# A planner that lets one engine at a time at a PSUM bank, a query copy moved to ScalarE, and matmuls without readers in TensorE's first waits

## The chip, the cores and the metric

One Trainium2 chip, one of its cores. The metric is the device time of one execution of the whole kernel in microseconds (us); of several runs the median counts.

## The reference, cut to what matters

The kernel computes three layers one after the other on 1536 tokens of width 512 (2 batches of 768): attention with 8 heads of width 64, where a query sees the first 4 keys and a window of 128 keys up to itself; a dense layer with a leaky maximum; and a layer of 8 experts, where each token with a positive skip score goes to the expert with the highest gate logit.

```python
def _attn_ref(q, k, v, n_sink, window):
    scores = scale * np.matmul(q, k.transpose(0, 1, 3, 2))
    ...
    keep = is_sink | in_window
    scores = np.where(keep, scores, -1000000000.0)
    ...
    a = a / (np.sum(a, axis=-1, keepdims=True) + 1e-09)
    return np.matmul(a, v).astype(np.float32)
def _moe_ref(x, w_in, w_out):
    h = x @ w_in
    g = np.maximum(0.01 * h, h)
    return (g @ w_out).astype(np.float32)
def _moe2_ref(x, w_skip, w_gate, w1, w2):
    ...
        h = np.maximum(xc[mask] @ w1[e], 0.0)
        y[mask] = gate_w[mask, None] * (h @ w2[e])
    out[do_compute] = xc + y
```

## The kernel before

**The work.** The tokens are cut into six groups of 256 (`NG`). For each group the heads are taken in four pairs (`KD`), and each pair in two query tiles of 128 (`item`, line 553). The dense layer runs over 16 chunks of 128 hidden columns for each group (`chunk`, line 832), and the attention of group g+1 is worked in between the chunks of group g. At the end come the experts (`plan_routed`, line 1035). Large products are split in a high and a low fp32r part: ScalarE (ACT) copies the high part out of PSUM, VectorE (DVE) subtracts it from the same PSUM tile and so makes the low part. Groups 0 and 1 (`whole`) use plain fp32 in attention, group 2 is `mixed`, groups 3 to 5 use split keys and queries.

**The planner.** The order in which instructions are issued is not that of the code. Every piece of work is an `Op` with an engine, a cost in ns by a small formula (`c_mm`, `c_act`, `c_dve`, lines 24 to 45), a priority, the tiles it reads and writes, and the operations it depends on. `Plan.run` (line 136) simulates the five engines: at each time each free engine takes the ready operation with the lowest priority number whose tiles fit in the free slots (`fits`, line 149). An operation becomes ready a fixed gap after the one it depends on ended: 195 ns after TensorE (PE), 150 ns after another engine. The start order of this simulation is the order in which the instructions are issued; each engine then works its own queue strictly in that order and waits at each instruction for what it needs. Two operations that only read the same tile have no dependency in the planner.

**PSUM.** There are 8 banks, by tag: 2 each for `acc`, `h` and `T`, 1 each for `S` and `PV` (line 245). Each tile of such a tag is one bank. Waits on the chip are put in by the tile framework from the issue order, not by the planner.

**The start.** `constants` (line 1337) runs first and is not in the plan: GpSimd (POOL) makes the identity `idt` and the tile `ones`; DVE waits for the loaded window limits and then makes the masks `mk` in some 13 instructions (lines 1351 to 1391). In the plan, `prep` (line 433) works one pair of group 0: PE transposes the keys into a `T` bank (line 450), ACT copies them out (454, 456), PE transposes the queries into the other `T` bank (460), and the two heads' queries, partitions 0 to 63 and 64 to 127 of that bank, are copied to `qz`, the first by ACT (468), the second by DVE (465, group 0 alone). Then `item` makes the scores (`score`, line 578), DVE masks them with their minimum (585), ACT takes the exponential (588), ACT or POOL divides by the sum (597, 600), PE transposes (616), ACT copies (620), PE multiplies by the values (655).

**Where two engines read one bank.** The query copies of group 0 (465, 468); the keys of groups 3 to 5, two ACT copies and two DVE subtractions (501, 503; `prep_keys`); the transposed weights of groups 2 to 5 (622, 623); the products with the values of groups 2 to 5 (670, 671). `idle` (line 825) already puts such matmuls without readers on the tile `self.spare` at the end of the dense layer:

```python
many = lambda: ones.rearrange("p (o n) -> p o n", o=1).to_broadcast([128, 4, 128])
for _ in range(n):
    self.p.op("PE", 216, lambda: nc.tensor.matmul(out=x.tile.rearrange("p (o n) -> p o n", o=4), lhsT=ones, rhs=many(), start=True, stop=True), w=[x], pr=self.KF * self.NG, after=[done])
```

Of the kernel before, what the change touches and what calls it, by code (L numbers as in the profile page):

```python
# [49 lines left out]


class Buf:
    __slots__ = ("tag", "shape", "dtype", "tile", "left", "state", "first", "loose")

    def __init__(self, tag, shape, dtype):
        self.tag, self.shape, self.dtype = tag, shape, dtype
        self.tile = None
        self.left, self.first = 0, 1 << 60
        self.state = {}


class Op:
    __slots__ = ("i", "eng", "cost", "fn", "pr", "after", "wait", "ready", "bufs", "lat", "start")


class Plan:
# [9 lines left out]
            return 0.0 if a.eng == "PE" else 125.0  # L76
        return 195.0 if a.eng == "PE" else 150.0

    def __init__(self, slots, any_order=()):
        self.any_order = any_order  # L80
        self.slots = dict(slots)
        self.tags = {}
        self.ops = []
        self.keys = {}
        self.gate = {}
# [11 lines left out]
    def op(self, eng, cost, fn, r=(), w=(), pr=0.0, lat=0.0, hold=(), after=()):  # L97

        o = Op()
        o.i, o.eng, o.cost, o.fn, o.pr, o.lat = len(self.ops), eng, cost, fn, pr, lat  # L100
        o.after, o.ready, o.start = [], 0.0, None
        deps, bufs = dict.fromkeys(after), {}
        for items, write in ((r, False), (w, True)):
            for it in items:
                base, sub = it if isinstance(it, tuple) else (it, None)
                if isinstance(base, Buf):
                    bufs[base] = None
                st = self._state(base)
                for s, (wr, rd) in st.items():
                    if sub is None or s is None or s == sub:  # L110
                        deps.update(dict.fromkeys(wr))
                        if write:
                            deps.update(dict.fromkeys(rd))
        for items, write in ((r, False), (w, True)):
            for it in items:
                base, sub = it if isinstance(it, tuple) else (it, None)
                st = self._state(base)
                if write:
                    if sub is None:
                        st.clear()  # L120
                    st[sub] = ([o], [])
                else:
                    st.setdefault(sub, ([], []))[1].append(o)
        deps.pop(o, None)
        o.wait = len(deps)
        for d in deps:
            d.after.append(o)
        bufs.update(dict.fromkeys(hold))
        o.bufs = list(bufs)
        for b in bufs:  # L130
            b.left += 1
            b.first = min(b.first, o.i)
        self.ops.append(o)
        return o

    def run(self, emit_alloc):
# [7 lines left out]
        def later(t, kind, x):  # L144
            nonlocal seq
            seq += 1
            heapq.heappush(future, (t, seq, kind, x))

        def fits(o):
            need = {}  # L150
            for b in o.bufs:
                if b not in taken:
                    if any(live.get(g, 0) for g in self.gate.get(b.tag, ())):
                        return False
                    n = need[b.tag] = need.get(b.tag, 0) + 1
                    if not b.loose and b not in turn[b.tag][0:n]:
                        return False
            return all(free[t] >= n for t, n in need.items())
# [5 lines left out]
        while future:  # L164
            now = future[0][0]
            while future and future[0][0] <= now:
                _, _, kind, x = heapq.heappop(future)
                if kind == "ready":
                    heapq.heappush(ready.setdefault(x.eng, []), (x.pr, x.i, x))
                elif kind == "done":  # L170
                    for d in x.after:
                        d.ready = max(d.ready, now + self.gap(x, d))
                        d.wait -= 1
                        if d.wait == 0:
                            later(d.ready, "ready", d)
                    for b in x.bufs:
                        b.left -= 1
                        if b.left == 0:
                            later(now + 100.0, "free", b)
                elif kind == "free":  # L180
                    free[x.tag] += 1
                    live[x.tag] -= 1
            for eng in sorted(ready):
                if engines.get(eng, 0.0) > now:
                    continue
                q, skipped, got = ready[eng], [], None
                while q:
                    item = heapq.heappop(q)
                    if fits(item[2]):
                        got = item[2]  # L190
                        break
                    skipped.append(item)
                for item in skipped:
                    heapq.heappush(q, item)
                if got is None:
                    continue
                for b in got.bufs:
                    if b not in taken:
                        taken.add(b)
                        if not b.loose:  # L200
                            turn[b.tag].remove(b)
                        free[b.tag] -= 1
                got.start = now
                order.append(got)
                engines[eng] = end = now + got.cost
                later(end, "idle", None)
                if got.lat:
                    dma_free = max(dma_free, now) + got.lat
                later(dma_free + 2000.0 if got.lat else end, "done", got)
# [16 lines left out]
class Arm:  # L226
# [4 lines left out]
    def __init__(self, tc, io, cst, scr, xg, window_attention):  # L231
# [16 lines left out]
        late = {"wm": 4, "xs": 3, "hs": 1, "gT": 1}  # L248
        self.psum_tags = ("acc", "h", "S", "T", "PV")
        self.base, self.attn, self.late = base, attn, late  # L250
        self.p = Plan({**base, **attn, **late}, ("T", "acc"))
        for t in late:
            self.p.gate[t] = tuple(attn)

# [178 lines left out]
    def prep(self, g, qp, p, whole):  # L433
# [21 lines left out]
        if qp == 0:  # L455
# [1 line left out]
        ks = lambda: self.ks[:, p:p + 1, :].to_broadcast([128, 2, 16])  # L457
        P.op("POOL", c_pool1(32), lambda: nc.gpsimd.tensor_scalar(
            out=snk(), in0=ks(), scalar1=1.0, scalar2=1.0, op0=ALU.mult, op1=ALU.mult), r=[("ks", p)], w=[(kT, "s")], pr=pr)
        P.op("PE", 2 * C_TR, lambda: [nc.tensor.transpose(pq.tile[:, j, :], flat("q", 2 * qp + j), idt) for j in range(2)],  # L460
             r=[part("q", 2 * qp + j) for j in range(2)], w=[pq], pr=pr, hold=[kT])
        for h in range(2):
            rows, key = slice(64 * h, 64 * h + 64), [(self.qz, (p % 2, h))]
            if g == 0 and h:
                P.op("DVE", c_dve(256), lambda rows=rows, h=h: nc.vector.tensor_scalar(
                    out=self.qz.tile[rows, p % 2, h, :], in0=pq.tile[rows].rearrange("p j c -> p (j c)"), scalar1=-0.125, scalar2=None, op0=ALU.mult), r=[pq], w=key, pr=pr)
            else:
# [278 lines left out]
    def plan_dense(self):  # L746
# [10 lines left out]
                self.split(self.xr[g, k], (xT, k), lambda i, k=k, xT=xT: xT.tile[:, i, k, :], 256, self.KF * g - 3, "ACT", "DVE")  # L757


        for _ in ahead(0):  # L760
            pass
        inputs(0)
# [36 lines left out]
        self.spare = self.p.buf("acc", [128, 512])  # L799
        self.idle(2, done)  # L800
        self.first_x(x2 + self.gating(g, acc, [1]))

    def first_rows(self):

# [639 lines left out]
```

## Time and profile before

| what | value |
|---|---|
| median of 3 runs | 550.58 us (549.27 to 551.24) |
| the profiled execution | 549.7 us, its span 548.0 us |
| TensorE busy | 517.1 us, 94% of the span |
| VectorE busy | 411.6 us, 75% |
| ScalarE busy | 344.3 us, 63% |
| GpSimd busy | 164.5 us, 30% |
| chain that ended last | PE 74%, DVE 11%, ACT 7%, issue 3% |

All rows are of the one profiled execution; its span runs from the first to the last instruction and is 1.7 us shorter than that execution's device time. Busy time of PE is modelled (matmuls overlap), so a PE that is busy is not one at its peak. An engine's "idle before" is the time in which its queue stood still ahead of an instruction, and the arrow names what ended that time. PEld is the weight load of TensorE, SPq and ACTq are the DMA issues of SyncE and ScalarE.

### The profile page before, as it was taken

Reading aid. Unit: us, or ns where it says so; the run is one execution under the profiler, and the core shown is the slowest. Engines: PE = TensorE matmul, PEld = TensorE weight load, DVE = VectorE, ACT = ScalarE, POOL = GpSimd, SP = SyncE. Lnnn points to the kernel's source line nnn. Section 1 sums busy time; section 2 is a strip of 40 time slices with the busy share of each in tenths; the row PEclk is TensorE's granted clock in tenths of the full one; section 3 lists DMA queues with packets and bytes.
Section 4 is the critical chain, followed back from the end, with each engine's and each line's share of the span. In section 5 each row is a group of like instructions: output and inputs, shape, how many; then the busy total and the mean of one; then the engine's idle time right before and its main releaser. Section 6 shows DMA issues by size and latency. Waiting matters only on the chain.

```text
span 548.0 us, 10288 instructions
## 1 busy us (share of the span) xinstructions
PE 517.1 (94%) x3341; PEld 452.8 (83%) x3341; DVE 411.6 (75%) x1168; ACT 344.3 (63%) x899; POOL 164.5 (30%) x288
## 2 busy tenths in 40 slices
PE   3889999999998999989999999999999999999994
PEld 2779899888887999878988889999998778888883
DVE  4889999998667677687777776675765587788781
ACT  3998865655576556676566676465656377765760
POOL 4332012230155134332433333211131033455331
PEclk9999999999999999999999999999999999999998
DMA  8998443630110211131112230104565359988750
GB/s 158 298 333 279 156 144 97 198 105 25 64 42 22 69 27 42 41 93 35 45 46 50 49 85 18 26 1 178 169 185 191 116 179 372 315 280 300 245 193 19
DMA packets 83806, 72.44 MB, mean 132 GB/s; under 512 B 56563, under 2 KB 64755, under 8 KB 83744
## 3 DMA queue, kind: packets, MB, share of 16 engines
q1 hardware_dynamic: 81456, 70.54, 42.3%
q0 software_dynamic: 1600, 1.04, 0.6%
q8 instruction: 28, 0.46, 0.3%
q14 instruction: 34, 0.28, 0.2%
q10 hardware_dynamic: 688, 0.13, 0.1%
HBM read 65.40 MB, written 10.51 MB: 139 GB/s over the span
## 4 chain that ended last, share of the span: by engine, by line
PE 74%; DVE 11%; ACT 7%; issue 3%; POOL 2%; DMA 2%; POOLq 0%; SPq 0%; ACTq 0%; DVEq 0%
PE h L845 19%; PE acc L866 15%; PE acc L1103 8%; PE h L1086 4%; PE PV L655 4%; PE T L616 3%; PE S L1086 2%; PE PV L1086 2%; PE S L582 2%; DVE C L671 2%; ACT P L588 2%; PE S L866 2%; PE PV L866 2%; DVE kT L503 1%; PE T L1096 1%
## 5 line engine op out<-in xcount | busy, mean ns | idle before, releaser
L845 PE MATMUL h<-x,w 128*128 128x256 f32 x1128 | 154.7, 286 | 0.3 <-DVE x L708 0.2
L845 PEld LDWEIGHTS h<-x,w 128*128 128x128 f32 x1128 | 144.1, 190 | 4.9 <-DVE w L708 0.6
L866 PE MATMUL acc<-w,gh 128*128 128x512 f32 x308 | 100.2, 406 | 0.0
L588 ACT ACTIVATE P<-P,s 128x272 f32<-128x272 f32 (+1 forms) x96 | 50.1, 523 | 27.6 <-DVE s L585 26.2
L600 POOL TENSOR_SCALAR P<-P,s 128x272 f32<-128x272 f32 (+1 forms) x72 | 36.6, 520 | 90.1 <-DVE s L593 77.4
L866 PE MATMUL acc<-w,gl 128*128 128x512 f32 x156 | 61.3, 393 | 0.0
L856 ACT ACTIVATE t<-h 128x256 f32<-128x256 f32 x94 | 35.6, 379 | 38.2 <-PE h L845 37.8
L866 PEld LDWEIGHTS acc<-w,gh 128*128 128x128 f32 x308 | 53.2, 189 | 7.6
L857 DVE TENSOR_TENSOR h<-h,t 128x256 f32<-128x256 f32 x94 | 40.2, 428 | 21.8 <-ACT t L856 21.2
L708 DVE TENSOR_TENSOR w<-wm,w 128x1024 fp32r<-128x1024 f32 x36 | 49.3, 1376 | 3.8 <-ACT w L701 3.2
L701 ACT ACTIVATE w<-wm 128x1024 fp32r<-128x1024 f32 x44 | 45.1, 1057 | 5.1 <-PE h L845 2.9
L859 DVE TENSOR_TENSOR gl<-h,gh 128x256 fp32r<-128x256 f32 x92 | 38.6, 419 | 10.2 <-ACT gh L858 8.9
L858 ACT ACTIVATE gh<-h 128x256 fp32r<-128x256 f32 x92 | 34.9, 379 | 17.4 <-DVE h L857 16.6
L585 DVE CUSTOM_DVE_ANT_0 P<-S,mk 128x272 f32<-128x272 f32 (+1 forms) x70 | 28.9, 413 | 14.7 <-PE S L582 10.2
L701 ACT ACTIVATE w<-wf 128x512 fp32r<-128x512 f32 x52 | 32.0, 626 | 11.1 <-DVE wf L741 8.8
L866 PEld LDWEIGHTS acc<-w,gl 128*128 128x128 f32 x156 | 29.3, 188 | 6.8 <-DVE gl L859 0.2
L708 POOL TENSOR_TENSOR w<-wm,w 128x1024 fp32r<-128x1024 f32 x8 | 19.7, 2461 | 41.8 <-ACT w L701 21.1
L616 PE MATMUL T<-idt,P 128*128 128x128 f32 x152 | 26.9, 293 | 3.8 <-DVE kT L503 2.9
L672 POOL TENSOR_TENSOR xr<-C 128x128 f32<-128x128 f32 x32 | 15.6, 488 | 47.2 <-DVE C L671 46.8
L708 DVE TENSOR_TENSOR w<-wf,w 128x512 fp32r<-128x512 f32 x42 | 28.8, 693 | 0.7 <-ACT w L701 0.7
L616 PEld LDWEIGHTS T<-idt,P 128*128 128x128 f32 x152 | 22.3, 205 | 8.5 <-issue 4.2
L622 ACT ACTIVATE AT<-T 128x256 fp32r<-128x256 f32 x60 | 20.1, 382 | 12.1 <-PE T L616 11.3
(274 smaller groups left out, 1105.9 us busy)
## 6 DMA issues: line engine op xcount, KB each, us to landing
wm<-in_moe_w_dram SPq DMA_DIRECT2D x44, 512.0 KB, 3.8
w<-in_moe_w_in_dram SPq DMA_DIRECT2D x14, 512.0 KB, 7.4
w<-in_moe_w_out_dram SPq DMA_DIRECT2D x14, 512.0 KB, 6.5
wf<-in_moe_w_dram SPq DMA_DIRECT2D x20, 256.0 KB, 4.4
vs<-in_moe_w_dram SPq DMA_DIRECT2D x10, 512.0 KB, 5.7
rq<-in_q_dram SPq DMA_DIRECT2D x56, 64.0 KB, 5.8
out_dram<-x SPq DMA_DIRECT2D x12, 256.0 KB, 2.5
rk<-in_k_dram SPq DMA_DIRECT2D x24, 96.0 KB, 2.2
```

Source lines behind the costliest of these rows:

```text
L588: P.op("ACT", 280 + 0.83 * ncol, lambda h=h: nc.scalar.activation(out=A.tile[:, 0:ncol, h], in_=A.tile[:, 0:ncol, h], func=AF.Exp, scale=- ...
L600: P.op("POOL", 245 + 0.83 * ncol, lambda h=h: nc.gpsimd.tensor_scalar(out=A.tile[:, 0:ncol, h], in0=A.tile[:, 0:ncol, h], scalar1=sm.tile[ ...
L616: nc.tensor.transpose(tt.tile[:, 2 * j + h, :], A.tile[:, o:o + 128, h], c["idt"])
L701: nc.scalar.activation(out=at(0), in_=view(src.tile), func=AF.Copy)
L708: P.op(lo, {"DVE": c_dve(n), "POOL": c_pool2(n)}[lo], lambda: eng[lo].tensor_tensor(out=at(1), in0=view(src.tile), in1=at(0).bitcast(F32), ...
L845: nc.tensor.matmul(out=h.tile, lhsT=wi.tile[:, a, 128 * k:128 * k + 128], rhs=xT.tile[:, b, k, :], start=k == 0 and n == 0, stop=k == self ...
L856: P.op("ACT", c_act(256, True), lambda: nc.scalar.activation(out=t.tile, in_=h.tile, func=AF.Copy, scale=0.01), r=[h], w=[t], pr=fast)
L857: P.op("DVE", c_dve(256), lambda: nc.vector.tensor_tensor(out=h.tile, in0=h.tile, in1=t.tile, op=ALU.max), r=[t], w=[h], pr=fast)
L859: P.op("DVE", c_dve(256), lambda: nc.vector.tensor_tensor(out=gl.tile, in0=h.tile, in1=gh.tile.bitcast(F32), op=ALU.subtract), r=[h, gh], ...
L866: nc.tensor.matmul(out=acc[i].tile, lhsT=a.tile[:, q], rhs=wo.tile[:, b, :], start=first and n == 0, stop=last and n == 2)
L1086: nc.tensor.matmul(out=hp[a].tile, lhsT=xt.tile[:, i, k, :], rhs=w1[k][j].tile[:, 512 * a:512 * a + 512], start=k == 0 and n == 0, stop=k ...
L1103: nc.tensor.matmul(out=yp.tile, lhsT=gt.tile[:, a, 2 * n + j, :], rhs=w2[n][b].tile[:, 512 * j:512 * j + 512], start=n == 0 and j == 0 and ...
```

## The change

Three edits. (1) The planner notes for each tile of a PSUM tag which engine last took it and until when (end plus 195 ns for PE, plus 150 ns for others); an operation of another engine on that tile does not fit before then. Operations that merely reserve a tile (`held`) don't count. (2) For the first pair of group 0 both heads' queries are copied by ACT; for pairs 1 to 3 the second head stays with DVE. (3) A function `warm` puts matmuls of `ones` with itself (bf16, 512 columns) on an `acc` tile that nothing reads: 7 at the head of TensorE's queue, 5 after the first pair's query transposes. The plan counts each at 10 ns.

```diff
 class Plan:
-    def __init__(self, slots, any_order=()):
-        self.any_order = any_order
+    def __init__(self, slots, any_order=(), banks=()):
+        self.any_order, self.banks = any_order, banks
...
+        o.held = set(hold) - set(bufs)
         bufs.update(dict.fromkeys(hold))
...
         def fits(o):
+            if any(b.tag in self.banks and b.by != o.eng and b.until > now and b not in o.held for b in o.bufs):
+                return False
             need = {}
...
                 later(end, "idle", None)
+                for b in got.bufs:
+                    if b.tag in self.banks and b not in got.held:
+                        b.by, b.until = eng, end + (195.0 if eng == "PE" else 150.0)
+                        later(b.until, "idle", None)
...
-        self.p = Plan({**base, **attn, **late}, ("T", "acc"))
+        self.p = Plan({**base, **attn, **late}, ("T", "acc"), self.psum_tags)
...
-        P.op("PE", 2 * C_TR, lambda: [nc.tensor.transpose(pq.tile[:, j, :], flat("q", 2 * qp + j), idt) for j in range(2)],
-             r=[part("q", 2 * qp + j) for j in range(2)], w=[pq], pr=pr, hold=[kT])
+        turned = P.op("PE", 2 * C_TR, lambda: [nc.tensor.transpose(pq.tile[:, j, :], flat("q", 2 * qp + j), idt) for j in range(2)],
+                      r=[part("q", 2 * qp + j) for j in range(2)], w=[pq], pr=pr, hold=[kT])
+        if g == 0 and p == 0:
+            self.warm(5, pr, [turned])
         for h in range(2):
             rows, key = slice(64 * h, 64 * h + 64), [(self.qz, (p % 2, h))]
-            if g == 0 and h:
+            if g == 0 and p and h:
                 P.op("DVE", c_dve(256), lambda rows=rows, h=h: nc.vector.tensor_scalar(
...
+        if self.fast:
+            self.spare = self.p.buf("acc", [128, 512])
+            self.warm(7, -100)

         for _ in ahead(0):
             pass
...
+    def warm(self, n, pr, after=()):
+        nc, ones, x = self.nc, self.c["ones"], self.spare
+        many = ones.rearrange("p (o n) -> p o n", o=1).to_broadcast([128, 4, 128])
+        self.p.op("PE", 10 * n, lambda: [nc.tensor.matmul(out=x.tile.rearrange("p (o n) -> p o n", o=4), lhsT=ones, rhs=many, start=True, stop=True) for _ in range(n)],
+                  w=[x], pr=pr, after=after)
```

## Rows read from the trace of the kernel before

**Rows 1.** Busy time by stage: stretch, length, each engine, PEclk, DMA share, GB/s.
```profile
8.30:20.00 11.70, 9.47 (x51) 7.60 (x52) 6.38 (x32) 8.71 (x33) 2.66 (x9) 1.00 1.08 277
20.00:56.00 36.00, 32.64 (x222) 28.10 (x222) 34.23 (x105) 32.31 (x99) 9.91 (x18) 1.00 1.00 294
56.00:166.00 110.00, 108.78 (x718) 97.25 (x717) 96.25 (x276) 69.63 (x196) 24.67 (x47) 1.00 0.33 101
166.00:380.00 214.00, 206.31 (x1442) 186.41 (x1441) 151.91 (x528) 133.10 (x409) 69.77 (x159) 1.00 0.18 46
```

**Rows 2.** The chain that ended last, its first 13 us: start, us, what.
```profile
0.91 4.07 DMA lim<-in_window_dram
...
8.02 0.30 DVE mk L1391
...
8.35 0.44 DVE w L465
```

**Rows 3.** The timeline of the start: start, us, instruction, idle before it.
```profile
2.24 0.19 POOL L1368 MEMSET ones<- 128x128 bf16 x1
...
5.72 0.99 PE L450 MATMUL T<-idt,w 128*128 128x128 f32 x2 [5.72 <-DMA w<-in_k_dram]
...
6.51 0.63 PE L460 MATMUL T<-idt,w 128*128 128x128 f32 x2
...
7.03 0.18 ACT L456 ACTIVATE ks<-T 128x16 f32<-128x16 f32 x1
...
8.81 0.38 ACT L468 ACTIVATE w<-T 64x256 f32<-64x256 f32 x1 [1.60 <-DVE w L465]
...
9.33 0.77 PE L578 MATMUL S<-kT,w 128*128 128x128 f32 x2 [2.19 <-ACT w L468]
...
10.14 0.29 DVE L585 CUSTOM_DVE_ANT_0 P<-S,mk 128x128 f32<-128x128 f32 x1 [1.36 <-PE S L578]
...
12.13 0.68 PE L450 MATMUL T<-idt,w 128*128 128x128 f32 x4
...
17.89 0.41 DVE L737 TENSOR_SCALAR wf<-w 128x512 int32<-128x512 int32 x1
```

**Rows 4.** Score matmuls to 12.6 us and from 15.5, line 830's (ns min/median/max).
```profile
L578 PE MATMUL S<-kT,w x4: 422/606/661, 9.3 to 11.7; 128*128 128x128 f32 x2, 128*128 128x272 f32 x2
...
L578 PE MATMUL h<-kT,w x6: 275/275/395, 15.7 to 17.8; 128*128 128x128 f32 x4, 128*128 128x272 f32 x2
...
L830 PE MATMUL acc<-ones x7: 376/389/393, 432.8 to 438.4; 128*128 128x512 bf16 x7
...
432.84 0.60 PE L830 MATMUL acc<-ones 128*128 128x512 bf16 x2
```

**Rows 5.** DMA before pair 1's transposes, columns as in rows 1, and the landing of weights.
```profile
10.00:10.50 0.50, 0.50 (x4) 0.50 (x4) 0.30 (x2) 0.03 (x1) 0.00 (x0) 1.00 1.31 208
...
11.00:11.50 0.50, 0.50 (x2) 0.38 (x2) 0.03 (x1) 0.40 (x2) 0.00 (x0) 1.00 0.43 87
...
10.44 0.58 SPq L720 DMA_DIRECT2D w<-in_moe_w_in_dram  x1
...
DMA to landing us min/median/max: 4.7/5.2/5.6
```

**Rows 6.** The timeline where ACT and DVE read one bank in a late group.
```profile
237.32 0.97 ACT L501 ACTIVATE kT<-T 64x384 fp32r<-64x384 f32 x2
238.33 1.12 DVE L503 TENSOR_TENSOR kT<-T,kT 64x384 fp32r<-64x384 f32 x2 [0.18 <-ACT kT L501]
```

**Rows 7.** The waits of PE from 166 to 380 us: us in total, times, longest.
```profile
PE T L616 <- DVE kT L503: 2.9, 7, 0.6
PE T L943 <- DVE wl L933: 1.3, 1, 1.3
PE T L638 <- DVE qT L684: 1.3, 4, 0.6
PE T L494 <- issue: 1.2, 1, 1.2
```

More of the change, by code (lines that the diff above doesn't have):

```diff
@@ L52 @@
 class Buf:
-    __slots__ = ("tag", "shape", "dtype", "tile", "left", "state", "first", "loose")
+    __slots__ = ("tag", "shape", "dtype", "tile", "left", "state", "first", "loose", "by", "until")
     def __init__(self, tag, shape, dtype):
@@ L58, in __init__ @@
         self.left, self.first = 0, 1 << 60
+        self.by, self.until = None, 0.0
         self.state = {}
 class Op:
-    __slots__ = ("i", "eng", "cost", "fn", "pr", "after", "wait", "ready", "bufs", "lat", "start")
+    __slots__ = ("i", "eng", "cost", "fn", "pr", "after", "wait", "ready", "bufs", "lat", "start", "held")
 class Plan:
```

## The prediction

> **What bounds the kernel now.** I read the busy time by stage first. From 56 to 166 us PE is busy for 108.78 of 110 us, from 166 to 380 us for 206.31 of 214 [rows 1]: there the end is set by TensorE's work and by its pauses, 7.7 us of them in the second stretch. Before that it is different. From 8.3 to 20 us no engine is full (PE 9.47 of 11.70, DVE 6.38, ACT 8.71), and from 20 to 56 us DVE (34.23 of 36) and ACT (32.31) are fuller than PE (32.64) [rows 1]. So the first 20 us are a chain of waits and not a full engine; what follows is work that moves as a whole if that chain gets shorter.
>
> Next the chain that ended last, in its first microseconds. It runs from the load of the limits through DVE's masks, which end at 8.02 + 0.30 = 8.32, to DVE's copy of the second head's queries (line 465) [rows 2]; ACT's copy of the first head's (line 468) comes right behind it, at 8.81 [rows 3]. These two copies write different parts of `qz` and only read one bank, yet ACT stood still for 1.60 us until DVE's was done, and the first scores began at 9.33 after PE had waited 2.19 us [rows 3]. So the program serializes readers of a bank, in the order of issue; DVE's copy came first in that order although DVE was busy with masks the planner doesn't know.
>
> The same in the late groups: ACT copies both heads' keys in 0.97 us from 237.32, and DVE's two subtractions, 1.12 us, start at 238.33, after the second ACT copy and not after the first [rows 6]. The planner believes that DVE can start after the first. For TensorE that ends in waits: of those from 166 to 380 us, 2.9 us in 7 places are for these subtractions, to get a free `T` bank, and 1.3 us in 4 for DVE's low part of the queries [rows 7].
>
> **The change part by part.** Sum against the profiled execution, 549.7 us (span 548.0); the median shown, 550.58, lies 0.88 above it.
>
> *The query copy of the first pair.* DVE loses 0.44 us [rows 2], which it did on the path; ACT gains a second copy of 0.38 [rows 3]. The transposes of the queries end at 6.51 + 0.63 = 7.14 and ACT is free at 7.03 + 0.18 = 7.21 [rows 3], so the copies run to about 7.6 and 8.0 instead of 9.2. Head 0's score needs only the first. Behind it nothing on ACT is hurt: its next work, the exponential, waits for DVE anyway.
>
> *The products without readers.* The seven can start when `ones` is made, 2.24 + 0.19 = 2.43 [rows 3], and read no load. Two products back to back take 0.60 us and one 0.389 [rows 4], so each adds 0.21 us at the fast rate. The first score matmuls took 422 ns (128 columns) and 661 (272), from 15.7 us on 275 and 395 [rows 4]: 239 against 120 ns for 144 more columns, twice. The granted clock reads 1.00 in all stretches [rows 1], that is the higher level of 1.2 and 2.4 GHz; the durations say that the first ones ran at the lower. At the slow rate a product adds 0.42 us and seven end at about 5.6. The keys' transposes can't start before 5.72, when the load lands [rows 3], so these seven cost nothing. The five lie between 7.14 and the score: at the fast rate to 8.2, inside the wait of 2.19 us that PE has there now; at the slow rate to 9.24, and the cover is gone. I take the fast rate, as seven products without a gap precede the transposes, where PE before had stood still for 5.72 us. DMA, SP and POOL issue nothing more; the `acc` bank that the products hold is wanted only by line 616, after the exponentials.
>
> *What the start gives.* Score at 8.2, its two matmuls 0.38 us, so DVE's line 585 at about 8.6 instead of 10.14: 1.5 us. The second tile's four matmuls of 272 columns run at the fast rate and save another 4 x 0.23 = 0.9 (272 columns at 120 ns for 144), so 2.4 us at the last score. Pair 1's transposes stand at 12.13 [rows 3]; the load rate falls from 208 GB/s at 10.0 to 87 at 11.0 [rows 5], so their data are in by about 10.5: at most 1.6 us earlier. The first weights are issued at 10.44 and land 5.2 us later [rows 5], 15.6, while DVE's decoding starts at 17.89 [rows 3]: room for 2.2. I take -1.6 us; the ends are -2.4 and 0, the latter if the products cover nothing and the later stages swallow the rest.
>
> Here the Trainium skill can be weighed. The page "PSUM — Partial Sum Buffer", section "PSUM bank collisions raise a hardware error", says that two engines may be in one bank at once when they touch different quadrants of 32 partitions; the two query copies do (0 to 63, 64 to 127). By it the 1.60 us would be no wait of the bank and the start would gain the clock's 0.9 alone, a sum of 548.2; the row shows the wait in this program, so the row decides.
>
> *The planner's exclusion.* It changes no instruction, only the order. A dependency already had the same gaps (195, 150), so only places with two concurrent readers move: 12 pairs of key copies, the four places listed in the kernel's description. Worked for the keys: the planner costs ACT's copy 52 + 0.83 x 384 = 371 ns and DVE's 465. Before, its bank was done at 371 + 150 + 2 x 465 = 1.45 us; now at 2 x 371 + 150 + 930 = 1.82. On the chip it takes 238.33 + 1.12 - 237.32 = 2.13 [rows 6]. The plan was 0.68 short and is now 0.31 short, so somewhat over half of the waits behind it should go: 1.5 of the 2.9 us [rows 7]. The wait for `T` shown as "issue" (1.2) and that for the queries (1.3) may go too, but their causes are other engines' lateness; I count nothing. The floor of this term is -4: 2.9 and half of the other two. Upward nothing excludes a loss, since every later choice of the planner can fall differently: I bound it by half the pauses of the stage with these places, 7.7 / 2 = +3.8.
>
> Sum: 549.7 - 1.6 - 1.5 = 546.6; plus 0.88, a median of 547.5 us.
>
> **The rivals.** A measurement of this kernel tells 0.3% from no change: below 548.9 is faster, above 552.2 slower.
>
> *Only the start counts.* The plan's new order gives back as much as it saves, as every operation behind the first moved one is chosen anew: 550.58 - 1.6 = 549.0. For it: waits other than those for the keys remain, such as 1.3 us for the gating's low part [rows 7].
>
> *The clock comes late.* If PE still runs slowly after the transposes, the five products end at 9.24 and the score starts at 9.3 as now. Only the 0.9 of the second tile is left; with half of the plan's term, 0.75, that is 548.9, without it 549.7. For it: the matmuls from 5.72 to 7.14 before were followed by slow ones [rows 3, 4]. Against it: the products fill the 3 us ahead of that.
>
> The page "TensorE: Matmul & The Clock Gate", Part 1, calls the half rate the default that sustained activity releases, at a point that varies from run to run; that speaks for this case, and the doubled durations agree.
>
> *The start is swallowed.* From 20 to 56 us DVE and ACT are at 95 and 90% [rows 1]; a shorter start could be met there by weights or slots that come no earlier, and the plan's term is nothing: 550.2.
>
> *Slower.* The exclusion holds a `T` bank 0.37 us longer in the plan, and with two such banks the planner puts the transposes of keys and of attention weights later; the attention of the next group then ends after the last chunk of the present one, and the first product of the group (line 845) waits for its input. It decides from 1.1 us per boundary on, in each of groups 3, 4 and 5: at 1.3, as the one gating wait [rows 7], 550.58 - 1.6 + 3.9 = 552.9.
>
> **How the numbers follow.** Forecast 0.52 (its own range 544.5 to 548.9); only the start 0.13, on the border, so half faster; late clock 0.08 and swallowed 0.12, no change; slower 0.15. Faster 0.52 + 0.06 = 0.58, same 0.27, slower 0.15. The range goes down to 550.58 - 2.4 - 4 = 544.2, say 544, and up to 551.5, past the neutral cases; what it leaves out is most of the slower case and a tail below.
>
> **What would show it.** Line 468 without a wait for DVE and done near 8.0; the first line 585 between 8.4 and 8.8; score matmuls of 275 and 395 ns from the first on; pair 1's transposes near 10.5; from 166 to 380 us fewer than 7.7 us of pauses and the wait of line 616 for 503 halved. The forecast is wrong if the start is 1.6 us earlier at 20 us but not at 56, if the first score stays near 9.3, or if PE's pauses after 166 us grow.

## The result, and the profile after

The changed kernel took 543.95 us (median of 4 runs, 541.82 to 544.02) against 550.65 us: the ratio is 0.9869, 95% interval [0.9845, 0.9893], 6.7 us less by the medians and 7.2 by the ratio. Forecast were 547.5 us and a range from 544.0 on: the direction was right, the gain more than twice the forecast one, and the result lies just below the range. The profiled execution took 543.89 us, its span is 542.2 (before 549.7 and 548.0).

Line numbers are higher now: by 8 to 10 up to line 750 (450 is 458, 460 is 468, 465 is 475, 468 is 478, 503 is 513, 578 is 588, 585 is 595, 616 is 626), and by 20 in the dense layer (845 is 865, 859 is 879).

First the busy time by stage of the changed kernel, columns as in [rows 1]; the number in brackets is that of the engine's instructions in the stretch:

```profile
8.30:20.00 11.70, 8.94 (x56) 7.04 (x55) 8.47 (x41) 11.00 (x41) 3.96 (x12) 0.97 1.05 274
20.00:56.00 36.00, 33.64 (x220) 29.05 (x219) 32.72 (x97) 30.83 (x92) 9.37 (x16) 0.96 1.04 310
56.00:166.00 110.00, 108.87 (x729) 98.25 (x727) 96.99 (x281) 69.42 (x197) 27.64 (x50) 1.00 0.32 96
166.00:380.00 214.00, 208.19 (x1465) 189.14 (x1465) 155.50 (x530) 134.41 (x412) 68.83 (x156) 1.00 0.20 52
```

From 166 to 380 us PE's pauses are 214 - 208.19 = 5.8 us instead of 7.7 [rows 1]. More telling is the count: PE worked 1465 matmuls there instead of 1442, and 729 instead of 718 from 56 to 166. It got through 34 more in the same time, while its busy time grew by only 1.9 and 0.1 us.

The start, as the timeline of the changed kernel shows it (start, us, instruction, idle before it):

```profile
2.49 3.17 PE L820 MATMUL acc<-ones 128*128 128x512 bf16 x7 [2.49 <-POOL ones L1388]
5.64 0.36 PE L458 MATMUL T<-idt,w 128*128 128x128 f32 x1
6.42 0.38 PE L468 MATMUL T<-idt,w 128*128 128x128 f32 x2
6.64 1.24 PE L820 MATMUL acc<-ones 128*128 128x512 bf16 x5
6.97 0.77 ACT L478 ACTIVATE w<-T 64x256 f32<-64x256 f32 x2
7.72 0.38 PE L588 MATMUL S<-kT,w 128*128 128x128 f32 x2
7.95 0.30 DVE L1411 TENSOR_SCALAR mk<-mk 128x272 f32<-128x272 f32 x1
8.17 0.28 DVE L595 CUSTOM_DVE_ANT_0 P<-S,mk 128x128 f32<-128x128 f32 x1
9.10 0.60 PE L458 MATMUL T<-idt,w 128*128 128x128 f32 x4
```

ACT copies both heads' queries without a wait; PE begins the first scores at 7.72 instead of 9.33, DVE's line 595 at 8.17 instead of 10.14, pair 1's transposes at 9.10 instead of 12.13 [rows 3]. Line 595 now follows directly on DVE's last mask (L1411). The score matmuls run at the higher rate from the first on; durations (ns min/median/max) of the S bank's first four, where [rows 4] had 422/606/661:

```profile
L588 PE MATMUL S<-kT,w x4: 273/334/393, 7.7 to 8.9; 128*128 128x128 f32 x2, 128*128 128x272 f32 x2
```

The clock's own entries in the traces agree with these durations. The first of them is the rise to the higher level, at 12.3 us in the kernel before and at 5.8 us in the changed one. (A table of stretches prints 1.00 ahead of the first entry too, so it can't show the slow start.)

PE's waits from 166 to 380 us (us in total, times, longest), against [rows 7]:

```profile
PE T L626 <- DVE kT L513: 1.9, 4, 0.8
PE h L865 <- DVE gl L879: 1.3, 2, 1.1
...
PE T L648 <- DVE qT L694: 0.5, 1, 0.5
```

The wait for the keys' subtractions fell from 2.9 us in 7 places to 1.9 in 4, those for the queries' low part at line 648 from 1.3 to 0.5 (with 0.6 at line 592 in addition), and the one marked "issue" is gone. A wait of the dense layer's product (L865) is new: it writes an `h` bank, and waits until DVE has read that bank for the low part of an earlier chunk (L879).

### The profile page after: what moved, and what is told of

It is laid out like the page before. It is cut to its first block, busy times and chain, and to the rows that moved or that the text cites. A ratio compares the mean times of both kernels' runs of the same rounds, so it can differ in the third digit from the quotient of the medians.

```text
span 542.2 us, 10303 instructions
## 1 busy us (share of the span) xinstructions
PE 517.6 (95%) x3353; PEld 453.3 (84%) x3353; DVE 413.3 (76%) x1167; ACT 343.6 (63%) x900; POOL 167.4 (31%) x288
## 3 DMA queue, kind: packets, MB, share of 16 engines
q0 software_dynamic: 1600, 1.04, 0.6%
## 5 line engine op out<-in xcount | busy, mean ns | idle before, releaser
L865 PE MATMUL h<-x,w 128*128 128x256 f32 x1128 | 155.6, 286 | 2.0 <-DVE gl L879 2.0
L865 PEld LDWEIGHTS h<-x,w 128*128 128x128 f32 x1128 | 144.2, 190 | 7.1 <-DVE gl L879 3.2
L610 POOL TENSOR_SCALAR P<-P,s 128x272 f32<-128x272 f32 (+1 forms) x72 | 39.5, 561 | 93.0 <-DVE s L603 75.8
L718 DVE TENSOR_TENSOR w<-wm,w 128x1024 fp32r<-128x1024 f32 x36 | 49.4, 1383 | 2.0 <-ACT w L711 1.7
L879 DVE TENSOR_TENSOR gl<-h,gh 128x256 fp32r<-128x256 f32 x92 | 38.5, 418 | 6.4 <-ACT gh L878 4.8
L718 DVE TENSOR_TENSOR w<-wf,w 128x512 fp32r<-128x512 f32 x42 | 29.2, 702 | 0.7 <-ACT w L711 0.7
L1030 POOL DMA_INDIRECT scr<-x,sm x12 | 13.2, 1098 | 50.6 <-ACT wl L969 16.0
L718 POOL TENSOR_TENSOR w<-wm,w 128x1024 fp32r<-128x1024 f32 x8 | 19.9, 2482 | 28.0 <-ACT w L711 22.0
L626 PE MATMUL T<-idt,P 128*128 128x128 f32 x152 | 25.8, 289 | 1.9 <-DVE kT L513 1.9
```

The lines of the kernel that those rows point to most:

```text
L610: P.op("POOL", 245 + 0.83 * ncol, lambda h=h: nc.gpsimd.tensor_scalar(out=A.tile[:, 0:ncol, h], in0=A.tile[:, 0:ncol, h], scalar1=sm.tile[ ...
L626: nc.tensor.transpose(tt.tile[:, 2 * j + h, :], A.tile[:, o:o + 128, h], c["idt"])
L718: P.op(lo, {"DVE": c_dve(n), "POOL": c_pool2(n)}[lo], lambda: eng[lo].tensor_tensor(out=at(1), in0=view(src.tile), in1=at(0).bitcast(F32), ...
L865: nc.tensor.matmul(out=h.tile, lhsT=wi.tile[:, a, 128 * k:128 * k + 128], rhs=xT.tile[:, b, k, :], start=k == 0 and n == 0, stop=k == self ...
L879: P.op("DVE", c_dve(256), lambda: nc.vector.tensor_tensor(out=gl.tile, in0=h.tile, in1=gh.tile.bitcast(F32), op=ALU.subtract), r=[h, gh], ...
```

## The experiments

Times are medians. The kernel before took between 549.89 and 551.03 us from session to session, so kernels are compared by their ratio to the before of their own session; a difference of 0.1% is 0.55 us.

### The two halves of the change

*Exclusion alone*: products and the query copy taken back.

```diff
-        if g == 0 and p == 0:
-            self.warm(5, pr, [turned])
...
-            if g == 0 and p and h:
+            if g == 0 and h:
...
-            self.spare = self.p.buf("acc", [128, 512])
-            self.warm(7, -100)
```

> The exclusion alone: the query copies of the first pair as before (ACT and DVE), no products without readers. Theory A (the planner's exclusion carries most, the start about 1.9 us of the 6.7): 545.5 to 547.5 us, so 3 to 5 below before, with the first score still at 9.3 and fewer pauses of PE between 166 and 380 us. Rival B (the start and the clock carry most, through everything behind them): 549 to 551.

Measured: 545.43 us, 0.992 [0.9899, 0.9941]. The start is as before: the copies still stand one behind the other, as the timeline of this run shows.

```profile
8.74 0.38 ACT L476 ACTIVATE w<-T 64x256 f32<-64x256 f32 x1 [1.61 <-DVE w L473]
8.86 0.76 PE L586 MATMUL h<-kT,w 128*128 128x128 f32 x2 [1.80 <-DVE w L473]
```

*Start alone*: the exclusion taken back; TensorE's matmuls, other than the products, then run in the order of before.

```diff
-        self.p = Plan({**base, **attn, **late}, ("T", "acc"), self.psum_tags)
+        self.p = Plan({**base, **attn, **late}, ("T", "acc"))
```

> The other two edits without the exclusion. Theory A: 548 to 549.5 us, 1.2 to 2.5 below before. Rival B: 543.5 to 545.5, nearly all of the gain.

Measured: 547.30 us, 0.9948 [0.993, 0.9966]. So the start is worth 0.52%, 2.9 us, and the exclusion 0.80%, 4.4 us; together 7.3, where the whole change gave 7.2 by its ratio. Within the intervals the two halves add up, and the larger one is that which the forecast had at 1.5.

*No products*: the exclusion and the copy, without the twelve products.

```diff
-        if g == 0 and p == 0:
-            self.warm(5, pr, [turned])
...
-            self.spare = self.p.buf("acc", [128, 512])
-            self.warm(7, -100)
```

> The changed kernel without the products that nobody reads (exclusion and both query copies on ACT). Theory A with the clock as the larger part of the start: 545 to 546, 1 to 2 above the changed kernel, the 272-column scores of the first pair at about 660 ns. If the products are worth nothing because the clock falls again at 19.4 us: 543.5 to 544.5. If they are most of the gain: over 547.

Measured: 544.67 us, 0.9896 [0.9879, 0.9914]: 0.15 to 0.27% above the whole change (0.9869, and 0.9881 when it was run again), and 0.24% below the exclusion alone. That lies between the ranges that were expected. By the middle values the products bring about 1 us and the copy about 1.3, but the intervals overlap, so only their sum is settled (the start alone, 2.9).

What the products do to the clock is settled by the traces. Without them its first entry, the rise, stands at 12.3 us (before), 13.3 (exclusion alone) and 17.1 us (no products); in all 17 profiled runs with them it stands between 5.5 and 7.8 us. Where it comes late the five products run slowly themselves and hold the scores up. In the run with ACT's price and the exclusion (below) the rise is at 7.8 us, and the timeline reads:

```profile
6.93 1.68 PE L820 MATMUL acc<-ones 128*128 128x512 bf16 x5
8.45 0.38 PE L588 MATMUL S<-kT,w 128*128 128x128 f32 x2
```

The scores start there 0.7 us later than in the profiled run of the change (7.72), and 0.8 later than in that without products (7.67), whose scores then ran at the lower rate.

### Where the exclusion's time comes from

From 56 to 380 us, one row of the busy time by stage for the kernel before:

```profile
56.00:380.00 324.00, 315.08 (x2158) 283.66 (x2157) 248.16 (x803) 202.74 (x604) 94.44 (x205) 1.00 0.23 65
```

for the start alone:

```profile
56.00:380.00 324.00, 314.93 (x2158) 283.64 (x2158) 247.68 (x801) 202.41 (x601) 94.84 (x205) 1.00 0.24 65
```

and for the whole change:

```profile
56.00:380.00 324.00, 317.07 (x2193) 287.39 (x2192) 252.49 (x810) 203.83 (x609) 96.47 (x205) 1.00 0.24 67
```

An earlier start leaves the pace as it was: 2158 matmuls in these 324 us. With the exclusion there are 35 more. PE's busy time grew by only 2.0 us, but that of its weight loads (the second number, PEld) by 3.7. The groups of instructions say which matmuls came in addition; before:

```profile
L845 PE MATMUL h<-x,w 128*128 128x256 f32 x913 | 125.1, 286 | 0.3 <-DVE x L708 0.2
...
L616 PE MATMUL T<-idt,P 128*128 128x128 f32 x136 | 24.2, 293 | 3.8 <-DVE kT L503 2.9 <-POOL P L600 0.6
```

and after:

```profile
L865 PE MATMUL h<-x,w 128*128 128x256 f32 x936 | 128.9, 286 | 2.0 <-DVE gl L879 2.0
...
L626 PE MATMUL T<-idt,P 128*128 128x128 f32 x136 | 23.2, 289 | 1.9 <-DVE kT L513 1.9
```

The attention's work is the same (136 transposes of weights in both), the dense layer is 23 products further. And the trap of the page can be read here: these products are listed at 286 ns each, but 936 of them at 286 would be 268 us, and the group's busy time is 128.9. A matmul's modelled time overlaps with that of the next, so a wait that is shorter than the overlap would leave no idle time in the table of waits.

How far the dense layer has come shows the gain in time. Durations (ns min/median/max) and the starts of the first and the last product of line 845 in an `h` bank, for the kernel before and for the exclusion alone:

```profile
L845 PE MATMUL h<-x,w x1128: 274/283/485, 25.1 to 423.2; 128*128 128x256 f32 x188
L862 PE MATMUL h<-x,w x1128: 274/283/482, 21.9 to 418.7; 128*128 128x256 f32 x188
```

The last one starts 4.5 us earlier, which is the whole gain; what follows it takes 124.8 and 124.9 us.

The page "Perfetto Trace Analysis" of the Trainium skill, section "Identifying the Most-Contended Engine", says that TensorE's matmul busy share is no good measure, since pipelined matmuls distort it, and advises the rate of the work done and the busy share of its weight loads instead. The traces agree: +2.0 us by the one, +3.7 by the other, 4.4 us measured.

### Rule or luck: five more pairs

One order that is better by 4 us could be luck, since the planner chooses everything behind its first moved operation anew. So its prices were nudged by amounts that mean nothing, each with and without the exclusion (the start edits in all):

```diff
-                            later(now + 100.0, "free", b)
+                            later(now + 130.0, "free", b)
```

> The start edits without the exclusion, and a planner nudged elsewhere: a slot counts as free 130 ns after its last use instead of 100. The nudge moves some 350 lines of TensorE's order and has no meaning of its own. Theory A (the exclusion makes the plan truer, whatever the order around it): 546 to 548.5 us, as the start alone had 547.3. Rival L (the changed kernel's order was a lucky draw and any reshuffle moves the time by some us either way): anything from 543 to 551.

> The changed kernel with the same nudge. Theory A: 3 to 5 us below its partner without the exclusion, so 542 to 545. Rival L: the difference to the partner is anywhere between -4 and +4; under 1.5 would speak for L.

```diff
 def c_dve(n):
-    return 66 + 1.04 * n
+    return 70 + 1.04 * n
```

> The start edits without the exclusion, another nudge: the planner's cost of a VectorE pass is 4 ns higher (70 instead of 66 plus 1.04 per element). Theory A: 546 to 548.5. Rival L: 543 to 551.

> The changed kernel with that second nudge. Theory A: 3 to 5 us below its partner, 542 to 545. Rival L: a difference under 1.5 in this pair or the other, or pairs of opposite sign.

```diff
-C_TR = 114.0
+C_TR = 118.0
```

> A neutral nudge (the planner's price of a transpose 118 ns instead of 114) with the start edits and without the exclusion. Theory A (the exclusion itself saves 3 to 5 us, whatever the order): 546.5 to 550, and 3 to 5 us above its partner with the exclusion. Rival L (the size is the luck of one order): the four orders so far without the exclusion went from 545.4 to 549.9 and those with it from 542.6 to 544.4, so L expects the partners of this pair and of the next to differ by under 2 us, or with the other sign, in at least one of them.

> The same nudge with the exclusion. Theory A: 542.5 to 545, 3 to 5 us below the partner. Rival L: within 2 us of the partner, or above it.

```diff
-    return (52 if psum else 93) + 0.83 * n
+    return (56 if psum else 97) + 0.83 * n
```

> Another neutral nudge (ScalarE's fixed cost 4 ns higher in the planner), without the exclusion. Theory A: 546.5 to 550. Rival L: anywhere from 543 to 550.

> The ScalarE nudge with the exclusion. Theory A: 542.5 to 545, 3 to 5 us below the partner. Rival L: within 2 us of the partner, or above it.

Measured, with PE's matmuls and the weight loads' busy us of 56 to 380 us from the busy time by stage (the last pair is the kernel before and the exclusion alone, times of their session):

| nudge | without: us, ratio | matmuls, loads | with: us, ratio | matmuls, loads | gain |
|---|---|---|---|---|---|
| none | 547.30, 0.9948 | 2158, 283.64 | 543.95, 0.9869 | 2193, 287.39 | 0.79% |
| slot delay | 549.92, 0.9997 | 2150, 282.45 | 544.42, 0.9918 | 2179, 285.64 | 0.79% |
| DVE's price | 545.44, 0.9908 | 2178, 285.30 | 542.63, 0.9872 | 2194, 287.84 | 0.36% |
| transpose's price | 548.36, 0.9953 | 2159, 282.60 | 543.89, 0.9891 | 2185, 287.39 | 0.62% |
| ACT's price | 550.84, 0.9996 | 2158, 283.05 | 545.74, 0.9892 | 2193, 287.37 | 1.04% |
| none, old start | 549.89, 1 | 2158, 283.66 | 545.43, 0.992 | 2193, 287.88 | 0.80% |

All six pairs gain, on average 0.73% or 4.0 us. (In the third the intervals, [0.9888, 0.9928] and [0.9833, 0.9911], overlap.) Rival L's signs, partners within 2 us of each other or a pair of the other sign, show in none. But theory A's figures were too narrow: 549.92, 545.44, 550.84 and 545.74 us lie outside their ranges, and the four nudged pairs differ by 2.8 to 5.5 us. Without the exclusion the orders lie from 545.4 to 550.8 us, with it from 542.6 to 545.7. So the gain is a property of the rule; how much of it one order shows is luck of some 2 us either way. The clock doesn't bring it: the mean granted clock of the timed runs was 0.993 to 0.996 in the kernels with the exclusion and 0.995 to 0.997 in those without. That the gain comes from a plan nearer to the program's waits, and not from something else that holding an engine back does, is argued and not shown.

In the profiled runs of all six pairs the last product of line 845 (865) starts earlier with the exclusion, by 2.3 to 4.9 us. What follows it differs by under 1 us within a pair, except under the slot delay (126.5 us without, where the clock stood at half for 3.4 us from 436.5 us on, and 124.7 with). Two orders without the exclusion took as long as the kernel before (0.9997 and 0.9996). Under ACT's price the start's gain still stands at that product (421.0 us, before 423.2) and is lost behind it, with and without the exclusion alike (127.2 us for the rest, before 124.8).

The pair under the slot delay also shows how little the table of waits tells. PE's wait for the keys' subtractions from 166 to 380 us, without and with the exclusion:

```profile
PE T L626 <- DVE kT L513: 1.4, 3, 0.6
PE T L626 <- DVE kT L513: 3.6, 6, 1.3
```

It grew, PE's busy time from 56 to 380 us went from 315.15 to 314.93 us, and yet 29 more matmuls got through and the kernel was 0.79% faster.

### Which banks

The forecast worked the exclusion for the keys alone, which lie in the T banks. So the rule was given the T tag alone, or the others alone:

```diff
-        self.p = Plan({**base, **attn, **late}, ("T", "acc"), self.psum_tags)
+        self.p = Plan({**base, **attn, **late}, ("T", "acc"), ("T",))
```

> The changed kernel, with the planner's exclusion for the T banks alone (keys, queries and transposed attention weights). If the waits for a T bank are what the exclusion saves: 543 to 545 us, as the changed kernel. If the products with the values (PV, one bank) carry it: 546.5 to 548, as the start edits alone.

```diff
+        self.p = Plan({**base, **attn, **late}, ("T", "acc"), ("PV", "S", "h", "acc"))
```

> The complement: the exclusion for PV, S, h and acc and not for T. If T carries it: 546 to 549. If PV does: 543 to 545. Both low would say that either is enough, or that the order decides more than the place.

and both again under the nudge of DVE's price:

> The exclusion at the T banks alone, under the nudge of DVE's price, whose form without any exclusion took 545.44 us and whose form with all of it 542.63. If T alone carries the gain: 542 to 543.5. If T alone brings nothing (as the run without a nudge said, 550.12): 545 to 550. If the two parts only work together: about 545.4.

> The exclusion at the banks other than T (PV, S, h, acc) under the same nudge. If these carry the gain: 542 to 543.5. If they bring nothing (as the run without a nudge said, 547.0 against 547.3): 545 to 547.

| exclusion at | no nudge | DVE's price |
|---|---|---|
| no bank | 0.9948, 2158 matmuls | 0.9908, 2178 |
| T | 1.0001 [0.9985, 1.0017], 2152 | 0.9985 [0.9966, 1.0003], 2143 |
| the others | 0.9942 [0.9921, 0.9963], 2173 | 0.991 [0.9887, 0.9933], 2172 |
| all | 0.9869, 2193 | 0.9872, 2194 |

The others alone bring nothing, T alone costs 0.53 and 0.77% (2.9 and 4.2 us), and both together gain. The parts don't add up, and T alone came out above every range expected of it, in both runs. The count of matmuls is a guide and no measure: the others alone got 15 more through than the start alone, and their last product of line 865 starts 2.2 us earlier (418.4 against 420.6 us), but what follows takes 1.7 us longer (126.4 against 124.7). With T alone the wait that the forecast priced does shrink, from 2.9 us and, under DVE's price, from 2.2, as PE's waits from 166 to 380 us show in the first of these runs

```profile
PE T L626 <- DVE kT L513: 1.9, 5, 0.6
```

and in the second:

```profile
PE T L626 <- DVE kT L513: 1.2, 3, 0.5
```

Yet both kernels are slower. The timeline of the first shows a place where it goes:

```profile
241.49 0.77 ACT L680 ACTIVATE C<-PV 64x256 f32<-64x256 f32 x2
...
242.28 0.38 ACT L693 ACTIVATE qT<-T 128x256 fp32r<-128x256 f32 x1
...
242.70 0.86 DVE L681 TENSOR_TENSOR C<-PV,C 64x256 f32<-64x256 f32 x2 [0.90 <-ACT qT L693]
243.59 0.42 DVE L694 SCALAR_TENSOR_TENSOR qT<-T,qT 128x256 fp32r<-128x256 f32 x1
...
244.16 0.63 PE L949 MATMUL T<-idt,x 128*128 128x128 f32 x4 [2.13 <-DVE qT L694]
```

DVE's additions for the values (L681) stood still for 0.90 us. They read the PV bank that ACT copies from (the old 670 and 671, a place that T alone doesn't cover). But these copies (L680) ended at 242.26, and the row names as the end of the wait ACT's copy of the queries (L693), which ended at 242.66; why the additions waited for that stays open. The queries' low part (L694) stood behind them in DVE's queue with a T bank in its hands, and PE waited 2.13 us for that bank. The whole change has the same wait of DVE, but PE had products of the dense layer to work on meanwhile:

```profile
239.43 0.88 PE L865 MATMUL h<-x,w 128*128 128x256 f32 x6
...
239.65 0.86 DVE L681 TENSOR_TENSOR C<-PV,C 64x256 f32<-64x256 f32 x2 [0.80 <-ACT qT L693]
```

With T alone, PE's clock fell to half behind that wait, as the busy time by stage shows (the third number from the end):

```profile
241.40:244.20 2.80, 0.67 (x9) 0.52 (x10) 1.60 (x5) 1.21 (x4) 2.27 (x6) 1.00 0.42 94
244.20:245.80 1.60, 0.95 (x7) 0.73 (x8) 0.61 (x3) 1.08 (x3) 1.07 (x3) 1.00 0.02 4
245.80:249.20 3.40, 3.40 (x18) 3.32 (x19) 2.34 (x8) 1.78 (x6) 0.38 (x3) 0.50 0.25 58
```

3.40 us at half the rate is 1.7 us of work lost; with the wait of 2.13 this place alone could account for the 2.9 us by which this kernel is behind the start alone. All its timed runs show the clock: its mean was 0.989 and, under DVE's price, 0.990, where the kernels without any exclusion had 0.996 and 0.997. The difference is 0.0065 in both before rounding, by estimate 0.0065 x 547 = 3.6 us of clock, about as much as the two losses. So T alone may lose by falls of the clock for the most part or wholly; what it would cost without them isn't shown. That the parts need one another because DVE has one queue for all banks fits the place, but isn't shown.

### Is a truer plan always a faster one?

The traces show ACT's and DVE's instructions longer than the planner's prices, and the gaps between engines shorter: a copy and a subtraction of [rows 6] took 485 and 560 ns where the plan has 371 and 465, and DVE began 40 ns behind ACT where it has 150. If the gain came from truth alone, correcting both should add to it:

```diff
+        if a.eng in ("ACT", "DVE"):
+            return 25.0 if a.eng == b.eng else 50.0
...
+        cost += 100.0 if eng in ("ACT", "DVE") and not lat else 0.0
...
-                        b.by, b.until = eng, end + (195.0 if eng == "PE" else 150.0)
+                        b.by, b.until = eng, end + (195.0 if eng == "PE" else 50.0)
```

> The changed kernel with one more truth in the plan: ACT's and DVE's operations cost 100 ns more and the gap behind them is 100 ns shorter, as the trace's durations have it (a 128x384 copy from PSUM takes 483 ns and the plan says 371, while the next engine starts some 45 ns after its end and the plan says 150). Theory A (a truer plan is a faster one): below the changed kernel, 540.5 to 543. Rival L (only the order's luck): 541 to 548 with no preference.

Measured: 575.57 us, 1.0473 [1.0446, 1.0501], outside both ranges. The idea falls in this form. From 166 to 380 us PE got through far less, with waits longer than any that the change has, at a mean clock of 0.95, which by itself is some 10 us of work (0.05 x 214); the row of the stretch, and the two longest waits from 20 to 380 us:

```profile
166.00:380.00 214.00, 195.40 (x1333) 173.51 (x1332) 148.91 (x546) 130.85 (x410) 76.44 (x172) 0.95 0.18 45
```

```profile
PE T L629 <- DVE sAT L655: 3.9, 2, 2.1
PE T L694 <- issue: 3.8, 1, 3.8
```

The kernel's priorities were set with the old prices; why these prices make it so much slower stays open.

### The clock's fall at 19 us

In the profiled run of the change PE waited 1.41 us for POOL, and the granted clock fell behind it:

```profile
19.30 1.13 PE L626 MATMUL acc<-idt,P 128*128 128x128 f32 x4 [1.41 <-POOL P L610]
```

```profile
18.00:19.40 1.40, 0.10 (x1) 0.10 (x2) 1.37 (x7) 1.40 (x5) 1.07 (x2) 1.00 1.30 260
19.40:22.80 3.40, 3.40 (x12) 2.78 (x13) 1.98 (x7) 2.00 (x5) 0.93 (x2) 0.50 1.23 213
```

To see whether that can be had back, four products of `ones` were to go ahead of that item's transposes, into the bank that these overwrite; and the change was run once more as it is.

```diff
         def tr():
+            if (g, p, qt) == (0, 2, 1):
+                for _ in range(4):
+                    nc.tensor.matmul(out=tt.tile, lhsT=ones, rhs=many, start=True, stop=True)
```

> The changed kernel with four more products of 512 columns ahead of the transposes of the third pair's second tile, where PE stood 1.4 us before its granted clock fell to 0.5 from 19.4 to 22.8 us. They write the bank that the transposes then overwrite. If that fall costs what 3.4 us at half rate cost on the path, 541.8 to 543.0 (1 to 2 below the changed kernel) and no stretch at 0.5 before 530 us. If ACT and DVE hide it: 543.5 to 544.5, the stretch gone all the same.

> The changed kernel once more, beside the three above on the same chip: 543 to 544.5 where its granted clock falls at 19.4 us, about 541.8 where it does not.

Measured: 542.99 us, 0.9871 [0.9851, 0.9891] with the products; 543.08 us, 0.9881 [0.9854, 0.9909] without. But the products missed the place, as the item named in the edit is another one. They ran at 25 us, and the wait still stands ahead of the transposes at 19.69:

```profile
19.69 0.74 PE L631 MATMUL acc<-idt,P 128*128 128x128 f32 x4 [1.42 <-POOL P L610]
...
24.99 1.04 PE L628 MATMUL acc<-ones 128*128 128x512 bf16 x4
```

At this place the run is thus one more of the change as it is. Its clock did not fall there:

```profile
19.40:22.80 3.40, 2.87 (x18) 2.37 (x19) 2.80 (x8) 2.61 (x7) 1.55 (x3) 1.00 1.39 220
```

Nor did it in the profiled run of the repeat, behind the same wait:

```profile
19.24 0.74 PE L626 MATMUL acc<-idt,P 128*128 128x128 f32 x4 [1.41 <-POOL P L610]
```

```profile
19.40:22.80 3.40, 3.15 (x23) 2.65 (x23) 2.85 (x9) 2.34 (x8) 1.29 (x2) 1.00 1.41 223
```

So the fall follows this wait in one profiled run of three, and whether products at the right place would keep it off wasn't tested. No version beats the change for certain (the nudge of DVE's price with the exclusion, 542.63 us, has an interval that takes in the change's).

## Why the prediction was wrong in size

**The step that failed** is the term of the planner's exclusion, -1.5 us; the runs give -4.0 on average of six pairs and -4.4 alone. The mechanism, two readers of a bank that the plan believed side by side, stood; its size was taken from the wrong quantity, in two ways. It was sized by half of the 2.9 us that PE's table of waits showed for the keys [rows 7]. That table holds only idle time that the overlapping, modelled matmuls leave over: 2.0 us of the gain show as fewer pauses of PE from 56 to 380 us, the rest only in the count of matmuls and the time of the weight loads, and under the slot delay this very wait grew with the gain. And it was worked for the keys as one of four places. With the rule at T alone that wait did shrink by a third and by nearly half (2.9 to 1.9, 2.2 to 1.2), and the kernel became slower; only all the places together gain. Which waits make up the 4 us stays open. That the term came out near its floor of -4 is luck, since the floor was added up from the same table.

**The query copy**: right. The wait of 1.60 us is gone, the copies end at 7.74 (forecast 8.0). The run with the exclusion alone shows that the wait comes from the program and not from the plan: it stood at 1.61 there.

**The products**: in the profiled run right that they cost nothing and that the first scores then run at the higher rate. The seven begin at 2.49 and the last ends at 5.66, as the keys' transposes start at 5.64; the five end at 7.88, modelled, and the score begins at 7.72. The rival of a late clock falls as a size, but its mechanism is real: the clock's rise comes between 5.5 and 7.8 us, and where it was late the five ran slowly and the scores began up to 0.7 us later (8.45). The clock of 1.00 that the prediction read for 8.3 to 20 us was in part a blank: the rise before is at 12.3 us. Its reading from the durations was the right one.

**The start's size**: -1.6 against -2.9 by the run with the start alone, beyond the end of -2.4. Line 595 came at 8.17 where 8.6 was forecast, because the transposes and copies ahead of it were earlier too (copies from 6.97, forecast 7.21), until DVE's masks set the end. The choice of 1.6 rested on a bound that did not hold: pair 1's data were said to be in by about 10.5, from the load rate, and its transposes ran at 9.10. The fall of the rate told here when the last data of the burst were in, not when those that were wanted had come.

**The rivals.** Only the start counts (549.0) and the start swallowed (550.2) both fall: the start alone was 547.30 us. Two orders without the exclusion did end where the kernel before does (0.9997 and 0.9996); in the second the start's gain was lost behind the dense layer and not from 20 to 56 us. The slower case falls too: what the dense layer's product waits for now, 2.0 us in 3 places from 20 to 380 us, is a free `h` bank (L879 reads it) and not its input. Only with the rule at T alone does it wait for its input (L718), for 1.1 and 0.9 us in all from 166 to 380 us.

**The range** left the result out by 0.05 us because its lower end was reached when both terms came out at their floors; the exclusion did, and the start went beyond, for separate reasons.

## What to carry to other kernels

Where a planner sets the order, it should know every rule by which the program will make one instruction wait for another, at all the places at once: here the rule at one tag alone cost 3 to 4 us, with a clock that fell more often, and the whole of it gained 4. Judge a change of order by several orders (nudge a price that means nothing, with and without the change), since two orders differed by over 5 us under prices that mean nothing. And on a full TensorE, compare how many matmuls two kernels get through in the same stretch, and when the last of a layer starts; its table of idle time showed under half of the gain. Look in the trace, too, whether an added instruction ran where it was meant to: here four products ran 5 us behind their place.

## What the hardware showed beside that

The granted clock fell from the higher to the lower level, 2.4 to 1.2 GHz, for 3.4 us: in the changed kernel at 19.4 us, behind a stretch in which PE was busy for 0.10 of 1.40 us, and with the exclusion at T alone at 245.8, behind stretches with 0.67 of 2.80 and 0.95 of 1.60. It doesn't fall in every run of the same program: behind the same wait of 1.41 us it stayed up in the repeat, and of the change's eight timed runs three had a mean clock of 0.995 or more and took 541.82, 542.27 and 542.36 us, five had 0.994 or less and took 543.80 to 544.21. That gap of about 1.8 us is near the 1.7 us that 3.4 us at half rate cost. The page "TensorE: Matmul & The Clock Gate" of the Trainium skill, Part 1, calls the half rate the default, which activity releases at a point that varies from run to run; these runs agree, with a rise between 5.5 and 7.8 us behind the same seven products, and they show that the fall varies as well. The twenty timed runs with the exclusion at T alone had 0.987 to 0.994, the four of the start alone 0.995 to 0.997: there the wait seems to have brought a fall nearly every time, as in both profiled runs.
